# Gated linear attention with a SiLU MLP on one core: opening re-ordered by half groups, weights behind the first inputs, logs a group ahead

## The chip, the cores and the metric

The kernel runs on one core of a Trainium2 chip. The metric is the device time of one execution in microseconds (us), lower is better. Besides the runs that are timed, one execution was recorded by the hardware profiler; its times are what the rest of this text reads.

The engines by their names in the profile: PE is TensorE (matmuls), PEld its weight loads, ACT is ScalarE (activations), DVE is VectorE, POOL is GpSimd, SP is SyncE, which here only issues DMAs. POOL and ACT can issue DMAs too. Every engine works through its own instructions in the order of the program.

## The reference

Four inputs of 4 x 8 x 768 x 48 floats (batch, heads, sequence, head size) go through a recurrence with a forget gate, and its output, as 3072 rows of 384, through a two-layer MLP.

```python
f = 1.0 / (1.0 + np.exp(-f_logit))
for t in range(S):
    state = f[:, :, t, :, None] * state + np.einsum('bhd,bhe->bhde', k[:, :, t], v[:, :, t])
    y[:, :, t] = np.einsum('bhd,bhde->bhe', q[:, :, t], state)
...
h = x @ w_in
g = h * (1.0 / (1.0 + np.exp(-h)))
return (g @ w_out).astype(np.float32)
```

## The kernel before

The sequence is cut into six groups of 128 positions; a group holds these positions for all four batches and eight heads (512 rows of the MLP). In a group the recurrence is computed as attention with decays, and a state of each batch goes from one group to the next. The work of a group g:

- `load(g)` (L74): four DMAs on SP's queue, in the order f, k, q, v, each 768 KB into tiles `f_ld`, `k_ld`, `q_ld`, `v_ld`, with two buffers each. A run of 48 floats (192 bytes) is contiguous in memory.
- `prep(g)`: ACT computes `e` = exp(-f) (L127) and `lf` = ln(1 + e) (L128) for the whole group. POOL copies v into `vp` (L130). Then, for each batch b, PE sums the logs along the positions into `cs` (L135), ACT makes `a` = exp(-cs) and `ia` = exp(cs) (L137, L139), DVE makes `qg` = q times `a` (L140), POOL makes `ki` = k times `ia` (L141). At the end PE sums the logs over the group (`al_ps`, L146) and ACT takes `al` of them (L150). Tiles `a` and `ia` have two buffers.
- `attend(g)`, for each batch: `transposes` (PE `t_ps` L169, DVE `qk` L171), `scores` (PE `a_ps` L179, DVE `atm` L183), `outputs` (PE `y_ps` L198, DVE `xT` L199) and `state` (PE `d_ps` L206 and L209, DVE `st` L213).
- `mlp_in(g)`: 16 tiles of three matmuls into `h_ps` (L240), each followed by ACT's SiLU into `hT` (L243). `mlp_out(g)`: 64 matmuls into `o_ps` (L250), DVE's copy to `o_sb` (L255), and the DMA out (L257).

Exp, Ln and SiLU each need their table on ACT; a change of table is an ACT_TABLE_LOAD in the profile.

The order on every engine is the order of the code, since the schedule is written by hand: `interleave` takes the next step of whichever stream has spent the smaller share of its stated cost. Ahead of the loop stand the constants, the clearing of `lf`, `qg`, `ki` (POOL, L94 to L96), `vp` and `st` (DVE, L97, L99), the two weight DMAs on POOL's queue (L102 `w_in_sb`, L104 `w_out_sb`), `load(1)`, `prep(0)`, and `attend(0)` interleaved with `prep(1)`. Then the loop over g: `load(g + 2)`; `mlp_in(g)` interleaved with the first half of `attend(g + 1)`; `mlp_out(g)` interleaved with its second half and with `prep(g + 2)`.

In PSUM one pool of three buffers, `acc`, holds `cs`, `al_ps`, `y_ps` and `d_ps` in turn; `t_ps` and `a_ps` have one buffer each; `h_ps` and `o_ps` share two.

Of the kernel before, what the change touches and what calls it, by code (L numbers as in the profile page):

```python
# [17 lines left out]
def interleave(*streams):  # L18


    live = [[g, float(total), 0.0] for g, total in streams]
    while live:
        s = min(live, key=lambda s: s[2] / s[1])
        try:
            s[2] += next(s[0])
        except StopIteration:
            live.remove(s)


@with_exitstack  # L30
def kernel(
# [10 lines left out]
    nc = tc.nc  # L42
# [17 lines left out]
    acc = ctx.enter_context(tc.tile_pool(name="acc", bufs=3, space=PSUM))  # L60
# [4 lines left out]
    def group_view(t, g):  # L65
        return t.rearrange("b h s d -> s (b h) d")[g * C:(g + 1) * C]

    loaded = {}

    def load(g):  # L70
        tiles = {}
        for name, src in (("f", f_logit), ("k", k), ("q", q), ("v", v)):
            t = ld.tile([C, B, H, D], F32, name=f"{name}_ld", tag=f"{name}_ld")
            nc.sync.dma_start(out=t.rearrange("p b h d -> p (b h) d"), in_=group_view(src, g))  # L74
            tiles[name] = t
        loaded[g] = tiles

    load(0)
# [9 lines left out]
    lf = [singles.tile([C, B, H, 64], BF16, name=f"lf{i}") for i in range(2)]  # L88
# [4 lines left out]
    for i in range(2):  # L93
        nc.gpsimd.memset(lf[i], 0.0)  # L94
        nc.gpsimd.memset(qg[i], 0.0)
        nc.gpsimd.memset(ki[i], 0.0)  # L96
        nc.vector.memset(vp[i], 0.0)  # L97
    for b in range(B):
        nc.vector.memset(st[b], 0.0)  # L99

    w_in_sb = singles.tile([128, KT, d_ff], BF16)
    nc.gpsimd.dma_start(out=w_in_sb, in_=moe_w_in.rearrange("(ko ki) n -> ki ko n", ki=128))  # L102
    w_out_sb = singles.tile([128, NT, d_model], BF16)
    nc.gpsimd.dma_start(out=w_out_sb, in_=moe_w_out.rearrange("(ko ki) n -> ki ko n", ki=128))  # L104

    load(1)

    def v_head(g, b, h):
        return 128 + h * VW

    def v_window(g, b, h, t):
        lo = v_head(g, b, h) - (h * D - t * 128)
        return vp[g % 2][:, b, lo:lo + 128]

    def st_block(b):
        base = st[b].rearrange("p n w -> p (n w)")
        return base

    alast = {}
    prepped = {}  # L120

    def prep(g):

        t = loaded.pop(g)
        i = g % 2
        e = gk.tile([C, B, H, D], F32, name="e")
        nc.scalar.activation(e, t["f"], AF.Exp, scale=-1.0)  # L127
        nc.scalar.activation(lf[i][:, :, :, 0:D], e, AF.Ln, bias=1.0)  # L128
        for b in range(B):
            nc.gpsimd.tensor_copy(  # L130
                vp[i][:, b, 128:].rearrange("p (h w) -> p h w", w=VW)[:, :, 0:D], t["v"][:, b])
        yield 0.0
        for b in range(B):
            cs = acc.tile([C, H, D], F32, name="cs", tag="acc")
            nc.tensor.matmul(cs, triu, lf[i][:, b, :, 0:D], start=True, stop=True)  # L135
            a = wk.tile([C, H, D], F32, name="a")
            nc.scalar.activation(a, cs, AF.Exp, scale=-1.0)  # L137
            ia = wk.tile([C, H, D], F32, name="ia")
            nc.scalar.activation(ia, cs, AF.Exp, scale=1.0)  # L139
            nc.vector.tensor_mul(qg[i][:, b, :, 0:D], t["q"][:, b], a)  # L140
            nc.gpsimd.tensor_mul(ki[i][:, b, :, 0:D], t["k"][:, b], ia)  # L141
            yield 162.0
        al_ps = acc.tile([C, B, NP], F32, name="al_ps", tag="acc")
        for b in range(B):
            for p in range(NP):
                nc.tensor.matmul(al_ps[:, b, p:p + 1], lf[i][:, b, 2 * p:2 * p + 2, :], ones,  # L146
                                 start=True, stop=True)
            yield 160.0
        al = gk.tile([C, B, NP], F32, name="al")
        nc.scalar.activation(al, al_ps, AF.Exp, scale=-1.0)  # L150
        alast[g] = al
        yield 0.0

    PREP = 4 * 162.0 + 4 * 160.0

    xT = {}

    def attend(g):
        i = g % 2
        x = gk.tile([128, KT, B, C], BF16, name="xT")  # L160
        xT[g] = x
        qk = {}
        atm = {}

        def transposes(b):
            t_ps = tps.tile([128, 2, NP, C], BF16, name="t_ps")
            for j, src in ((0, qg), (1, ki)):
                for p in range(NP):
                    nc.tensor.transpose(t_ps[:, j, p, :], src[i][:, b, 2 * p:2 * p + 2, :], ident)  # L169
            sb = wk.tile([128, 2, NP, C], BF16, name="qk")  # L170
            nc.vector.tensor_copy(sb, t_ps)  # L171
            qk[b] = sb

        def scores(b):
            a_ps = aps.tile([C, 2, NP, C], F32, name="a_ps")
            for p in range(NP):
                for r in range(2):
                    lo = 64 * r
                    nc.tensor.matmul(a_ps[:, r, p, :], qk[b][lo:lo + D, 1, p, :], qk[b][lo:lo + D, 0, p, :],  # L179
                                     start=True, stop=True)  # L180
            sb = wk.tile([C, 2, NP, C], BF16, name="atm")
# [141 lines left out]
```

## Time and profile before

| | |
|---|---|
| median of three runs | 272.38 us (271.5 to 273.1) |
| the profiled execution | 272.63 us |
| its span, first to last instruction | 270.6 us |
| mean granted TensorE clock | 0.943 |
| busy: PE, ACT, DVE, POOL | 197.8, 125.3, 108.1, 49.3 us |
| read from and written to memory | 25.17 MB and 4.72 MB |

The profiled execution's time is 2.0 us more than its span. How to read the views used below: the slices cut the span into 40 equal parts and give busy tenths of each engine. The chain that ended last goes back from the last instruction, at each step to what released it; in order of time it reads as the path on which the end depends. The timeline gives instructions in order (start, duration, engine, line, operation), and in brackets how long the engine stood idle before them and what released it. The view by windows gives, for a stretch, its length, then busy time of PE, PEld, DVE, ACT, POOL with instruction counts, the granted TensorE clock (1.00 is full), the DMA share and GB/s. The groups by line give shapes, counts, busy time and mean ns of one.

### The profile page before, as it was taken

The numbers are of one execution on the slowest core, as the hardware profiler recorded it, in microseconds if no ns is written. First come the engines' busy times: TensorE is split into PE (matmuls) and PEld (weight loads), VectorE is DVE, ScalarE is ACT, GpSimd is POOL, SyncE is SP. The second block draws the span as 40 slices with busy tenths as digits, with TensorE's granted clock in tenths as the row PEclk, the third lists the DMA queues.
The fourth block names the chain that finished last, engine by engine and source line by source line (L and its number), as shares of the span: only waits on it lengthen the run. The fifth ranks groups of instructions, "written<-read, shape, count | busy, mean of one in ns | idle before, by whom it ended". The sixth has DMA issues, their size and how long they took to land.

```text
span 270.6 us, 3905 instructions
## 1 busy us (share of the span) xinstructions
PE 197.8 (73%) x1616; PEld 117.7 (44%) x1632; DVE 108.1 (40%) x191; ACT 125.3 (46%) x184; POOL 49.3 (18%) x64
## 2 busy tenths in 40 slices
PE   0120003567993999975999939999849999999995
PEld 0010002455552575542664525755426655664352
DVE  7420020965243555432743434644327443720011
ACT  1910039023669415678236695156783266105700
POOL 9900070260200410004400006200044000000000
PEclk9999999995997799997999977999959999999999
DMA  9999999999000015991119980159920100011011
GB/s 145 186 207 191 184 200 186 187 183 189 7 1 0 33 58 112 167 197 23 51 39 201 187 109 29 39 115 187 189 26 30 61 29 4 0 61 58 0 48 69
DMA packets 104626, 26.99 MB, mean 100 GB/s; under 512 B 99104, under 2 KB 104224, under 8 KB 104608
## 3 DMA queue, kind: packets, MB, share of 16 engines
q1 hardware_dynamic: 102144, 23.60, 55.9%
q0 software_dynamic: 2464, 3.15, 6.6%
q8 instruction: 12, 0.20, 0.4%
q14 instruction: 6, 0.05, 0.1%
HBM read 25.17 MB, written 4.72 MB: 110 GB/s over the span
## 4 chain that ended last, share of the span: by engine, by line
PE 64%; SPq 15%; ACT 9%; DMA 4%; DVE 4%; issue 1%; POOL 1%; POOLq 0%
PE o_ps L250 25%; PE h_ps L240 23%; SPq L74 15%; PE y_ps L198 6%; DMA v_ld<-in_v_dram 4%; PE t_ps L169 4%; PE a_ps L179 2%; ACT lf L128 2%; ACT e L127 2%; ACT L128 2%; ACT L127 2%; PE cs L135 2%; DVE atm L183 1%; DVE qk L171 1%; PE d_ps L206 1%
## 5 line engine op out<-in xcount | busy, mean ns | idle before, releaser
L243 ACT ACTIVATE hT<-h_ps 128x512 bf16<-128x512 f32 x96 | 57.3, 597 | 45.7 <-PE h_ps L240 43.8
L250 PE MATMUL o_ps<-w_out_sb,hT 128*128 128x384 bf16 x384 | 77.3, 348 | 0.0
L240 PE MATMUL h_ps<-xT,w_in_sb 128*128 128x512 bf16 x272 | 73.1, 383 | 1.4 <-issue 0.2
L250 PEld LDWEIGHTS <-hT 128*128 128x128 bf16 x384 | 37.3, 103 | 44.4 <-issue 26.4
L140 DVE TENSOR_TENSOR qg<-q_ld,a 128x384 bf16<-128x384 f32 x24 | 15.1, 632 | 60.3 <-ACT a L137 48.3
L240 PEld LDWEIGHTS <-w_in_sb 128*128 128x128 bf16 x288 | 25.8, 98 | 27.5 <-issue 5.9
L135 PE MATMUL cs<-lf,triu 128*128 128x384 bf16 x24 | 10.0, 434 | 37.2 <-ACT lf L128 35.3
L171 DVE COPY qk<-t_ps 128x1024 bf16<-128x1024 bf16 x24 | 16.6, 691 | 45.0 <-PE y_ps L198 38.0
L130 POOL CAST vp<-v_ld 128x384 bf16<-128x384 f32 x24 | 11.5, 519 | 125.7 <-DMA v_ld<-in_v_dram 125.7
L183 DVE TENSOR_TENSOR atm<-a_ps,triu 128x512 bf16<-128x512 f32 x48 | 30.8, 684 | 4.9 <-PE a_ps L179 4.7
L141 POOL TENSOR_TENSOR ki<-k_ld,ia 128x384 bf16<-128x384 f32 x24 | 24.3, 1022 | 33.5 <-ACT ia L139 33.5
L169 PE MATMUL t_ps<-ident,ki 128*128 128x128 bf16 x96 | 10.5, 238 | 21.5 <-POOL ki L141 21.5
L255 DVE COPY o_sb<-o_ps 128x384 f32<-128x384 f32 x24 | 13.4, 558 | 29.5 <-PE o_ps L250 29.2
L198 PE MATMUL y_ps<-atm,vp 128*128 128x128 bf16 x240 | 23.5, 231 | 1.2 <-DVE xT L199 1.1
L139 ACT ACTIVATE ia<-cs 128x384 f32<-128x384 f32 x24 | 11.7, 486 | 25.1 <-POOL ki L141 24.9
L137 ACT ACTIVATE a<-cs 128x384 f32<-128x384 f32 x24 | 11.8, 491 | 20.8 <-PE cs L135 18.9
L213 DVE TENSOR_TENSOR st<-d_ps,al 48x192 bf16<-48x192 f32 x40 | 14.1, 353 | 14.1 <-PE d_ps L209 13.8
L198 PEld LDWEIGHTS <-vp 128*128 128x128 bf16 x240 | 17.6, 104 | 1.8 <-issue 1.6
L150 ACT ACTIVATE al<-al_ps 128x16 f32<-128x16 f32 x6 | 1.1, 183 | 34.4 <-PE al_ps L146 34.4
L169 PEld LDWEIGHTS <-ki 128*128 128x128 bf16 x96 | 7.3, 107 | 21.7 <-POOL ki L141 21.7
L198 PE MATMUL y_ps<-qk,st 128*128 128x128 bf16 x120 | 16.5, 219 | 0.0
L169 PEld LDWEIGHTS <-qg 128*128 128x128 bf16 x96 | 8.1, 106 | 17.6 <-issue 12.4
(34 smaller groups left out, 152.1 us busy)
## 6 DMA issues: line engine op xcount, KB each, us to landing
f_ld<-in_f_logit_dram SPq DMA_DIRECT2D x6, 768.0 KB, 6.9
k_ld<-in_k_dram SPq DMA_DIRECT2D x6, 768.0 KB, 10.3
q_ld<-in_q_dram SPq DMA_DIRECT2D x6, 768.0 KB, 10.9
v_ld<-in_v_dram SPq DMA_DIRECT2D x6, 768.0 KB, 11.2
out_dram<-o_sb SPq DMA_DIRECT2D x24, 192.0 KB, 1.9
w_in_sb<-in_moe_w_in_dram POOLq DMA_DIRECT2D x1, 1536.0 KB, 11.6
w_out_sb<-in_moe_w_out_dram POOLq DMA_DIRECT2D x1, 1536.0 KB, 21.5
```

What stands on the lines that cost most here:

```text
L74: nc.sync.dma_start(out=t.rearrange("p b h d -> p (b h) d"), in_=group_view(src, g))
L135: nc.tensor.matmul(cs, triu, lf[i][:, b, :, 0:D], start=True, stop=True)
L140: nc.vector.tensor_mul(qg[i][:, b, :, 0:D], t["q"][:, b], a)
L141: nc.gpsimd.tensor_mul(ki[i][:, b, :, 0:D], t["k"][:, b], ia)
L169: nc.tensor.transpose(t_ps[:, j, p, :], src[i][:, b, 2 * p:2 * p + 2, :], ident)
L171: nc.vector.tensor_copy(sb, t_ps)
L183: nc.vector.tensor_mul(sb[:, r], a_ps[:, r], triu[:, None, :].to_broadcast([C, NP, C]))
L198: nc.tensor.matmul(y_ps[:, t, :], l, r, start=(n == 0), stop=(n == len(terms) - 1))
L213: nc.vector.tensor_mul(blocks[lo:lo + D, :, r * D:(r + 1) * D], d_ps[lo:lo + D, :, r * D:(r + 1) * D], alast[g][lo:lo + D, b, :, None].to_ ...
L240: nc.tensor.matmul(h_ps, w_in_sb[:, kk, n * 128:(n + 1) * 128], xT[g][:, kk].rearrange("p b c -> p (b c)"), start=(kk == 0), stop=(kk == K ...
L243: nc.scalar.activation(hT[g][:, n, :], h_ps, AF.Silu)
L250: nc.tensor.matmul(o_ps, hT[g][:, n, b * C:(b + 1) * C], w_out_sb[:, n, :], start=(n == 0), stop=(n == NT - 1))
```

## The change

1. **Loads.** `load` takes a group, a name and a range of batches. Group 0 is loaded in two halves (batches 0 and 1, then 2 and 3); f and q of it are issued by SP, k and v by ACT. From group 2 on, f of a group is loaded an iteration ahead of its k, q and v.
2. **Weights.** The two weight DMAs become four (512 columns of `w_in` each) and two (half of `w_out` each), and POOL issues them later in its order, `w_in` behind the second half's `ki`, `w_out` behind its `vp`.
3. **Clearing.** Only the last 16 of 64 columns of `lf`, `qg`, `ki` are cleared, by DVE; `st` and the second `vp` are cleared by POOL behind the weight DMAs.
4. **Order of group 0.** Its `prep` and `attend` run by halves, without interleaving with group 1; its `state` steps are interleaved with `prep(1)`.
5. **Logs a group ahead.** `logs(g)` (`e` and `lf`) is taken out of `prep`, and runs on ACT behind the second phase of iteration g - 3 (`lf` gets a third buffer). For group 2 it runs at the start of the second phase of iteration 0, and there `prep(2)` starts only when 5000 of its 6250 cost units have passed.
6. **In `prep`.** `ia` comes before `a`; `vp` and `ki` alternate on POOL; all `al_ps` matmuls stand together.
7. **PSUM.** `acc` (3) is split into `cps` (1 buffer for `cs` and `al_ps`) and `yps` (2 for `y_ps` and `d_ps`). Tile `qk` gets a third buffer.
8. **Stated costs** of the attend steps change from 560, 450, 1100, 450 to 450, 350, 900, 330.

The diff, cut to this:

```diff
-    acc = ctx.enter_context(tc.tile_pool(name="acc", bufs=3, space=PSUM))
+    cps = ctx.enter_context(tc.tile_pool(name="cps", bufs=1, space=PSUM))
+    yps = ctx.enter_context(tc.tile_pool(name="yps", bufs=2, space=PSUM))
...
+    def load(g, name, b0=0, b1=B, eng=None):
+        if (g, name) not in loaded:
+            loaded[g, name] = ld.tile([C, B, H, D], F32, name=f"{name}_ld", tag=f"{name}_ld")
+        t = loaded[g, name]
+        src = SRC[name].rearrange("b h s d -> s (b h) d")[g * C:(g + 1) * C, b0 * H:b1 * H]
+        (eng or nc.sync).dma_start(out=t[:, b0:b1].rearrange("p b h d -> p (b h) d"), in_=src)
+
+    HB = B // 2
+    for lo, hi, names in ((0, HB, "fkqv"), (HB, B, "fkqv")):
+        for name in names:
+            load(0, name, lo, hi, nc.scalar if name in "kv" else nc.sync)
...
+    def load_w_in():
+        src = moe_w_in.rearrange("(ko ki) n -> ki ko n", ki=128)
+        for n in range(0, d_ff, 512):
+            nc.gpsimd.dma_start(out=w_in_sb[:, :, n:n + 512], in_=src[:, :, n:n + 512])
...
+    def logs(g, lo, hi):
...
+        nc.scalar.activation(e[:, lo:hi], f[:, lo:hi], AF.Exp, scale=-1.0)
+        nc.scalar.activation(lf[g % 3][:, lo:hi, :, 0:D], e[:, lo:hi], AF.Ln, bias=1.0)
+
+    def decay(g, b):
+
         i = g % 2
...
+        cs = cps.tile([C, H, D], F32, name="cs", tag="cs")
+        nc.tensor.matmul(cs, triu, lf[g % 3][:, b, :, 0:D], start=True, stop=True)
+        ia = wk.tile([C, H, D], F32, name="ia")
+        nc.scalar.activation(ia, cs, AF.Exp, scale=1.0)
+        nc.gpsimd.tensor_mul(ki[i][:, b, :, 0:D], loaded[g, "k"][:, b], ia)
+        a = wk.tile([C, H, D], F32, name="a")
+        nc.scalar.activation(a, cs, AF.Exp, scale=-1.0)
+        nc.vector.tensor_mul(qg[i][:, b, :, 0:D], loaded[g, "q"][:, b], a)
...
+    def prep(g, wait):
+
+        yield wait
+        for b in range(B):
+            values(g, b)
+            decay(g, b)
+            yield 200.0
+        lasts(g)
+        yield 450.0
...
     with tc.manual_schedule():
...
+        logs(0, 0, 1)
+        logs(0, 1, HB)
+        for half in range(2):
+            mine = range(half * HB, half * HB + HB)
+            if half:
+                logs(0, HB, B)
+            for b in mine:
+                decay(0, b)
+            for b in mine:
+                transposes(0, b)
+            if half:
+                load_w_in()
+            for b in mine:
+                values(0, b)
+            for b in mine:
+                scores(0, b)
+            if half:
+                load_w_out()
+                pads(lf[1], qg[1], ki[1], lf[2])
+                for b in range(B):
+                    nc.gpsimd.memset(st[b], 0.0)
+                nc.gpsimd.memset(vp[1], 0.0)
+                for name in "fkqv":
+                    load(1, name)
+            for b in mine:
+                outputs(0, b)
+        lasts(0)
+        logs(1, 0, B)
+        for _ in interleave_gen((prep(1, 0.0), prep_cost(0.0)), (chain(*[once(state, 0, b) for b in range(B)]), B * 330.0)):
             pass
...
+        load(2, "f")
+
         for g in range(NCH):
             if g + 2 < NCH:
...
+                for name in "kqv":
+                    load(g + 2, name)
+            if g + 3 < NCH:
+                load(g + 3, "f")
...
             if g + 2 < NCH:
...
+                wait = 0.0
+                if g == 0:
+                    logs(2, 0, B)
+                    wait = 5000.0
+                second.append((prep(g + 2, wait), prep_cost(wait)))
...
+            if g + 3 < NCH:
+                logs(g + 3, 0, B)
```

**ACT in the opening.** The rows of ACT's order from the start of the program, before; `lf_105` is the `lf` of group 0, the numbers mark buffers.

```order
L127 ACT_TABLE_LOAD
L127 ACTIVATE e<-f_ld 128x1536
L128 ACT_TABLE_LOAD
L128 ACTIVATE lf_105<-e 128x32x48
L137 ACT_TABLE_LOAD
L137 ACTIVATE a<-cs 128x384
L139 ACTIVATE ia<-cs 128x384
```

And now, from the same place (`lf_112` is group 0's):

```order
L85 DMA k_ld<-in_k_dram 128x16x48
L85 DMA v_ld<-in_v_dram 128x16x48
L85 DMA k_ld<-in_k_dram 128x16x48
L85 DMA v_ld<-in_v_dram 128x16x48
L142 ACT_TABLE_LOAD
L142 ACTIVATE e<-f_ld 128x384
L143 ACT_TABLE_LOAD
L143 ACTIVATE lf_112<-e 128x8x48
L142 ACT_TABLE_LOAD
L142 ACTIVATE e<-f_ld 128x384
L143 ACT_TABLE_LOAD
L143 ACTIVATE lf_112<-e 128x8x48
```

Four DMA issues now stand ahead of ACT's first table load, and the first half's logs are taken batch by batch, with four table loads where one pair stood.

**POOL in the opening.** Before, behind the constants (`vp_111` and `ki_109` belong to group 0):

```order
L94 MEMSET lf_105 128x2048
L95 MEMSET qg_107 128x2048
L96 MEMSET ki_109 128x2048
L94 MEMSET lf_106 128x2048
L95 MEMSET qg_108 128x2048
L96 MEMSET ki_110 128x2048
L102 DMA w_in_sb<-in_moe_w_in_dram 128x3x2048
L104 DMA w_out_sb<-in_moe_w_out_dram 128x16x384
L130 CAST vp_111<-v_ld 128x8x48 x4
L141 TENSOR_TENSOR ki_109<-k_ld,ia 128x8x48 x4
```

And now (`ki_117`, `vp_119` of group 0, `vp_120` of group 1):

```order
L152 TENSOR_TENSOR ki_117<-k_ld,ia 128x8x48 x2
L158 CAST vp_119<-v_ld 128x8x48 x2
L152 TENSOR_TENSOR ki_117<-k_ld,ia 128x8x48 x2
L119 DMA w_in_sb<-in_moe_w_in_dram 128x3x512 x4
L158 CAST vp_119<-v_ld 128x8x48 x2
L124 DMA w_out_sb<-in_moe_w_out_dram 128x8x384 x2
L324 MEMSET st_121 128x1536
L324 MEMSET st_122 128x1536
L324 MEMSET st_123 128x1536
L324 MEMSET st_124 128x1536
L325 MEMSET vp_120 128x6144
L158 CAST vp_120<-v_ld 128x8x48
```

The weight DMAs moved behind both halves' `ki`, and five memsets stand between them and the first work on group 1.

**ACT in a middle iteration.** Before, behind the sixteen SiLUs of `mlp_in(1)`, up to those of `mlp_in(2)` (`lf_106` is group 3's):

```order
L243 ACTIVATE hT<-h_ps 128x512 x16
L127 ACT_TABLE_LOAD
L127 ACTIVATE e<-f_ld 128x1536
L128 ACT_TABLE_LOAD
L128 ACTIVATE lf_106<-e 128x32x48
L137 ACT_TABLE_LOAD
L137 ACTIVATE a<-cs 128x384
L139 ACTIVATE ia<-cs 128x384
```

And now, the end of the same stretch (`lf_113` is now group 4's), behind the four pairs of `ia` and `a` of `prep(3)`:

```order
L151 ACTIVATE ia<-cs 128x384
L154 ACTIVATE a<-cs 128x384
L167 ACTIVATE al<-al_ps 128x16
L142 ACTIVATE e<-f_ld 128x1536
L143 ACT_TABLE_LOAD
L143 ACTIVATE lf_113<-e 128x32x48
L261 ACT_TABLE_LOAD
L261 ACTIVATE hT<-h_ps 128x512 x16
```

The logs moved from between the SiLUs and the exponentials of the same `prep` to between the last exponential and the next group's SiLUs, for the group after.

256 lines of the change are left out of this document (119 added, 137 removed).

## The prediction

> **What bounds the kernel now.** I read the slices first, then the chain in order of time, then the windows by stage, then single rows. The slices of the granted clock and of DMA:
>
> ```profile
> PEclk9999999995997799997999977999959999999999
> DMA  9999999999000015991119980159920100011011
> ```
>
> A slice is 6.8 us. DMA is full for ten slices, to 68 us, and later only in bursts. The clock dips after the opening and again once in every group. The chain says what the first 64 us are:
>
> ```profile
> 0.74 0.43 SPq L74
> ...
> 1.23 3.09 SPq L74
> ...
> 12.76 15.56 SPq L74
> ...
> 40.97 10.99 DMA v_ld<-in_v_dram
> ...
> 52.53 1.74 POOL vp L130 x3
> 54.27 0.97 POOL ki L141
> ...
> 64.27 0.59 PE h_ps L240
> ```
>
> SP's issues stall (0.43 us for the first, up to 15.56 later) until v of **group 1** lands at 51.96; then 12.3 us of one group's preparation run until the first `h_ps` at 64.27 (call this start S). From there the stages, each ending where the next group's `h_ps` begins:
>
> ```profile
> 36.00:52.10 16.10, 5.74 (x49) 4.02 (x50) 6.23 (x10) 9.09 (x13) 5.24 (x8) 1.00 1.45 187
> 64.30:103.50 39.20, 34.05 (x278) 20.18 (x282) 17.21 (x34) 22.00 (x32) 5.83 (x8) 0.88 0.17 33
> 103.50:140.80 37.30, 32.25 (x277) 19.35 (x280) 16.97 (x33) 21.31 (x32) 5.83 (x8) 0.95 0.65 107
> 140.80:178.50 37.70, 32.65 (x277) 19.42 (x280) 17.05 (x33) 21.32 (x32) 5.90 (x8) 0.91 0.68 105
> 178.50:216.20 37.70, 32.62 (x278) 19.49 (x281) 17.05 (x33) 21.39 (x32) 5.83 (x8) 0.91 0.68 105
> 216.20:245.10 28.90, 28.05 (x238) 16.85 (x241) 12.07 (x21) 9.76 (x17) 0.00 (x0) 1.00 0.08 29
> 245.10:270.60 25.50, 22.07 (x110) 10.56 (x109) 2.55 (x5) 9.56 (x16) 0.00 (x0) 1.00 0.10 39
> ```
>
> PE fills the later stages, except for one hole in each of the four groups that prepare another. That of the second, from ACT's and PE's timelines:
>
> ```profile
> 118.44 0.60 ACT L243 ACTIVATE hT<-h_ps 128x512 bf16<-128x512 f32 x1 [0.49 <-PE h_ps L240]
> 119.06 1.28 ACT L127 ACT_TABLE_LOAD   x1
> 120.35 1.48 ACT L127 ACTIVATE e<-f_ld 128x1536 f32<-128x1536 f32 x1
> 121.85 1.28 ACT L128 ACT_TABLE_LOAD   x1
> 123.15 1.48 ACT L128 ACTIVATE lf<-e 128x1536 bf16<-128x1536 f32 x1
> ...
> 124.68 0.32 PE L135 MATMUL cs<-lf,triu 128*128 128x384 bf16 x1 [4.73 <-ACT lf L128]
> 124.84 2.32 PE L250 MATMUL o_ps<-w_out_sb,hT 128*128 128x384 bf16 x8
> ...
> 127.28 1.49 PE L250 MATMUL o_ps<-w_out_sb,hT 128*128 128x384 bf16 x4
> 128.56 0.40 PE L206 MATMUL d_ps<-st,ident 128*128 128x384 bf16 x1
> ...
> 256.73 10.45 PE o_ps L250 x64
> ```
>
> PE stands 4.73 us at `cs` for the logs, and is slow behind it: the twelve `o_ps` took 2.1 and 1.3 us where 64 of them take 10.45, so 12 take 1.96; with two `cs` that is 1.7 us lost. A group without hole is therefore 37.3 - 4.7 - 1.7 = **30.9 us**. The 28.9 of the stage at 216.2, with no `prep` or state, is the cross-check.
>
> **The change, part one: the start S.** Three chains end there; none is simply removed.
>
> *Data.* Up to the last byte of group 1 the same bytes must move. The first 12 us ran at 163 GB/s and later ones at 187, so data begin at about 1.5 us:
>
> ```profile
> 0.00:12.00 12.00, 0.74 (x3) 0.50 (x4) 8.09 (x7) 6.31 (x5) 11.43 (x14) 1.00 1.18 163
> ...
> q0 software_dynamic: 959, 0.74, 93.5%
> q1 hardware_dynamic: 956, 0.18, 33.5%
> ```
>
> A 768 KB load is 4.2 us at 187 GB/s, a group 16.8; group 0 lands at 18.3. To 51.96 before, that leaves 51.96 - 1.5 - 33.6 = 16.9 us for the weights. The last two rows are the weight queue and the input queue in the stretch 24 to 29 us: both move the same number of packets, so they alternate, and a weight packet is many times larger. Now `w_in` is cut into runs of 512 columns: 1536 + 2048 = 3584 weight packets, beside which 3584 input packets of 192 bytes (3.7 us alone) pass. If POOL issues the weights at T, group 1 has had T - 18.3 of its 16.8 us. For T = 31, 4.1 us are left, more than 3.7: all weights go first, and v lands at 52 as before. For T = 33, 2.1 us are left (2050 packets), v lands at 33 + 2.1 + 16.9 x 2050/3584 = 45; from T = 35 on, at once. So **later weights bring S forward**.
>
> As to ACT as a second issuer: the DMA share was 1.45 on one queue already. The Trainium skill ("DMA: Bandwidth & Descriptors", Issuing engines are not separate DMA queues) says that DMAs started on several engines run on the same engines and interleave; by it the second queue brings nothing, against some 8 us earlier for group 0 if it doubled the rate. The full share speaks for the rule. My sum goes by the share alone.
>
> *ACT and PE.* Durations, from the groups by line:
>
> ```profile
> L141 POOL TENSOR_TENSOR ki<-k_ld,ia 128x384 bf16<-128x384 f32 x24 | 24.3, 1022 | 33.5 <-ACT ia L139 33.5
> ...
> L130 POOL CAST vp<-v_ld 128x384 bf16<-128x384 f32 x24 | 11.5, 519 | 125.7 <-DMA v_ld<-in_v_dram 125.7
> ...
> L183 DVE TENSOR_TENSOR atm<-a_ps,triu 128x512 bf16<-128x512 f32 x48 | 30.8, 684 | 4.9 <-PE a_ps L179 4.7
> ...
> L140 DVE TENSOR_TENSOR qg<-q_ld,a 128x384 bf16<-128x384 f32 x24 | 15.1, 632 | 60.3 <-ACT a L137 48.3 <-DMA q_ld<-in_q_dram 11.8
> ...
> L139 ACT ACTIVATE ia<-cs 128x384 f32<-128x384 f32 x24 | 11.7, 486 | 25.1 <-POOL ki L141 24.9
> L135 PE MATMUL cs<-lf,triu 128*128 128x384 bf16 x24 | 10.0, 434 | 37.2 <-ACT lf L128 35.3 <-ACT ia L139 1.1 <-DVE xT L199 0.8
> ...
> L94 POOL MEMSET lf<- 128x2048 bf16 x2 | 3.6, 1796 | 0.0
> ...
> L102 POOL DMA_DIRECT2D w_in_sb<-in_moe_w_in_dram x1 | 0.9, 931 | 0.0
> ```
>
> ACT's four issues block it until its ring takes them. Bounds: 2 us (a first issue on SP takes 0.43 us) and 14 us (the pace of the data); I take 7.5, since SP's second issue waited 3 us. Then per batch of the first half two table loads (1.28) and two activations of about 0.45: to 14.4. Table load, `ia`, `a`, `cs`, `ia`, `a`: to 18.1. From there DVE and PE for two batches: `qg`, `qk`, transposes, `qk`, scores, `atm` pair, scores, `atm` pair, outputs, eight steps of 0.6 to 1.4: the second half's `cs` at 26. Its table load waits for it; then 4.2 us to the last `ki`: **T = 31**. Behind this the second half's attention ends at 38, and only then ACT takes the logs of group 1 (4.4 us with the Ln load): 43. `prep(1)`, four `cs` one after another through one PSUM buffer, 1.4 us each, with the table load, ends near **52**.
>
> *POOL.* At T it issues `w_in` four times (0.93 each), copies `vp`, issues `w_out` twice (taken alike), then clears 4 x 1536 + 6144 columns at 1.796 us for 2048: 10.8 us, until 48.4. Two `vp` and `ki` pairs for group 1 (3.1), the last `ia` and `a`, `al_ps` and a state (2.0): **53.5**. Data, with v at 52, gives 52 + 3.1 + 2.0 = **57**, or 50 with v at 45. I take S = **55**, near the middle of 52, 53.5 and 57. Bounds: 50 (late weights and an ACT freed at 2 us) and 60 (ACT freed at 14). Gain 9.3.
>
> **Part two: the four groups** (39.2 + 37.3 + 37.7 + 37.7 = 151.9).
>
> ```profile
> 105.72 1.29 PE h_ps L240 x6
> ...
> 131.84 0.89 PE y_ps L198 x16
> ```
>
> - *Groups 2 and 3* find their logs ready. In place of the hole ACT's Exp table load now waits for the first `cs`: 1.28 + 0.39 + 0.49 = 2.2 us until the one `cs` buffer is free, while PE has eight `o_ps` (1.3): 1.0 us is left, 31.9 each. The logs stand behind `al`: 1.5 + 1.3 + 1.5 + 1.3 = 5.6 us on ACT, and the first SiLU must end (0.6) before the third `h_ps` tile finds a buffer. Until there PE has 20 `o_ps` (3.3), an `y_ps` (0.9), a `d_ps` (0.5), two `h_ps` tiles (1.3) and their transposes (0.9): 6.9 against 6.2, covered, barely.
> - *Group 0*: `prep(2)` is pressed into the last fifth of the second phase. There `cs` waits for `ia` and `a` of the one before: 1.6, 1.1, 0.4 and 0.5 us, 3.6 together, and the cold start of before (1.5, from 39.2 against 37.7) stays, with 0.5 for slow matmuls: 36.5.
> - *Group 1* starts with ACT still at the logs of group 3 (5.6 us behind `al`), and `h_ps` has two buffers: PE has four `o_ps`, two `h_ps` tiles and two transposes (2.8), then waits, with DVE's copies between, 3.5 us for the first SiLU. With 1.5 for the clock behind it and 1.0 as above: 36.9.
>
> As to that 1.5: the clock behind the 4.73 us was
>
> ```profile
> 125.00:130.00 5.00, 5.00 (x30) 2.55 (x28) 2.29 (x5) 2.70 (x6) 2.64 (x4) 0.66 0.02 5
> ```
>
> The Trainium skill ("TensorE: Matmul & The Clock Gate", What's actually happening) says the clock halves after at least one idle window of about 3.4 us, which runs freely. By it the row is explained, waits of 1 us cost nothing more, and one of 3.5 us may or may not: the sum would be 1.5 lower if it does not.
>
> Sum 36.5 + 36.9 + 31.9 + 31.9 = 137.2; gain 14.7. The last two stages (54.4) hold the same work: nothing.
>
> **Total**: 55 + 137.2 + 54.4 = 246.6 of span, plus 2.0 around it (272.63 against 270.6): **249 us**. The profiled execution stands 0.25 us over the median of 272.38, which I neglect.
>
> **The rivals.**
> - *An early opening*: T falls to 33 or later, or group 1 comes in ahead of the weights; then the chains of 50 to 52 decide, and short waits leave the clock alone: 249 - 5 - 3 = 241. For it: the steepness above. Against: POOL's memsets alone reach 48.4. Chance 0.15.
> - *The opening is not shortened*: POOL's six issues or ACT's four block longer than I took; S stays near 64, 258 in all. For it: SP's issue of 15.56 us in the chain. Against: the one large weight issue took 0.93 us. Chance 0.15.
> - *The logs do not leave the path* (the change doesn't do what it says): the cover of 6.9 us against 6.2 fails, and groups 2 and 3 also start with a wait for SiLU, 3.5 + 1.5 each: 259. Chance 0.10.
> - *Slower*: with the holes gone, PE runs densely from S on, and the granted clock sinks under the load. 191.6 us follow S; the gain of 24 is gone when they stretch by 24/191.6, a mean clock of 0.89; at 0.85 the time is 249 + 34 = 283. For it: 0.88 to 0.95 in the groups. Against: the last 54 us, with PE busy 28.05 of 28.9 us, ran at 1.00, and the dips lie behind holes. Chance 0.04.
>
> **How the numbers follow.** The forecast has 0.56. The range goes from 240 (the early case) to 259 (the two late ones); the slower case and the far ends stay out. A difference of 0.5% (1.4 us, about the spread of the runs) is what can be told from no change. Faster 0.95, same 0.02, slower 0.03 (of the 0.04 a little falls into no change, and the late cases stay faster).
>
> **What would show it.** Right: first `h_ps` at 52 to 58; no 4.7 us hole at `cs`; waits of about 1 us at the second `cs` of groups 2 and 3; a wait of 3 to 4 us for SiLU at the start of group 1; weights issued near 31; v of group 1 near 50. Wrong: ACT's first `e` later than 14 us, POOL standing in its DMA issues, or `h_ps` waits at the starts of groups 2 and 3.

## The result: the profile after

| | before | after |
|---|---|---|
| median of the runs | 271.94 us (271.06 to 273.10) | 252.75 us (249.62 to 252.91) |
| ratio, 95% interval | | 0.9265 [0.9183, 0.9346] |
| the profiled execution | 272.63 us | 252.69 us |
| its span | 270.6 us | 250.9 us |
| mean granted TensorE clock | 0.943 | 0.984 |

The prediction was 249, with a range of 240 to 259. Where the runs of a kernel fell into a fast and a slow state, as in one experiment below, its ratio is that of the fast runs alone. The slices of the granted clock and of DMA after the change (6.3 us each):

```profile
PEclk9999999999999999599999999999999999999998
DMA  9999999999980107992017993159801100110011
```

DMA is full for eleven slices, to 69 us (the weights now come last), and of four dips of the clock behind holes one is left, near 100 us. (Up to 61.8 us the trace has no record of the clock, and the view puts 1.00 there; the last section comes back to this.) The windows by stage, cut at each group's first `h_ps` (length; busy time of PE, PEld, DVE, ACT, POOL; granted clock; DMA share; GB/s):

```profile
0.00:58.04 58.04, 17.14 (x160) 12.25 (x162) 22.81 (x37) 25.73 (x36) 27.93 (x34) 1.00 1.33 182
58.04:94.48 36.44, 32.57 (x277) 19.73 (x279) 18.44 (x34) 21.29 (x32) 7.23 (x9) 1.00 0.60 95
94.48:132.50 38.02, 33.57 (x279) 19.79 (x280) 18.70 (x34) 23.62 (x33) 8.03 (x10) 0.91 0.64 105
132.50:164.40 31.90, 30.57 (x280) 18.75 (x281) 18.37 (x33) 19.91 (x31) 6.81 (x8) 1.00 0.80 124
164.40:196.30 31.90, 30.57 (x279) 18.75 (x281) 18.38 (x33) 17.11 (x29) 6.81 (x8) 1.00 0.61 100
196.30:225.30 29.00, 28.68 (x240) 17.17 (x243) 12.91 (x22) 9.55 (x16) 0.00 (x0) 1.00 0.08 28
225.30:250.90 25.60, 21.96 (x110) 10.48 (x108) 2.44 (x5) 9.56 (x16) 0.00 (x0) 0.97 0.11 39
```

Read the lengths against the prediction's terms. S came at 58.04 for 55; groups 0 to 3 took 36.44, 38.02, 31.90 and 31.90 for 36.5, 36.9, 31.9 and 31.9; the last two stages 54.6 for 54.4. The chain in order of time (start, duration, what) says what the first stage was made of:

```profile
0.74 0.49 ACTq L85
1.26 2.07 ACTq L85
3.36 4.87 ACTq L85
8.26 4.45 ACTq L85
12.74 1.28 ACT L142
...
36.32 0.91 POOL w_in_sb L119 x2
...
42.18 5.34 POOL st L324 x4
47.52 5.16 POOL vp L325
52.75 0.76 POOL vp L158
...
58.04 1.06 PE h_ps L258 x2
```

ACT's four DMA issues hold it until 12.74; then comes the chain of decays and scores; POOL issues the weights, clears `st` and `vp` for 10.5 us, and only then works on group 1. No DMA stands in the chain any longer: v of group 1 (issued at 25.34, landed 11.1 us later) is there long before POOL comes to it at 52.75. The idle times of PE, from its timeline, which were 4.73 us in each of four groups:

```profile
89.41 0.32 PE L149 MATMUL cs<-lf,triu 128*128 128x384 bf16 x1 [1.65 <-ACT a L154]
90.75 0.32 PE L149 MATMUL cs<-lf,triu 128*128 128x384 bf16 x1 [1.02 <-ACT a L154]
92.09 0.32 PE L149 MATMUL cs<-lf,triu 128*128 128x384 bf16 x1 [0.37 <-ACT a L154]
93.44 0.54 PE L164 MATMUL al_ps<-ones,lf 128*128 128x1 bf16 x16 [0.69 <-ACT a L154]
...
100.32 2.72 PE L258 MATMUL h_ps<-xT,w_in_sb 128*128 128x512 bf16 x6 [3.19 <-ACT hT L261]
...
119.94 0.32 PE L149 MATMUL cs<-lf,triu 128*128 128x384 bf16 x1 [1.00 <-ACT a L154]
```

and three windows around the 3.19:

```profile
99.00:99.50 0.50, 0.00 (x0) 0.00 (x0) 0.00 (x0) 0.50 (x1) 0.00 (x0) 0.88 1.40 218
100.30:105.30 5.00, 4.98 (x22) 2.02 (x22) 1.29 (x2) 1.94 (x4) 0.00 (x0) 0.50 1.45 188
106.00:106.50 0.50, 0.50 (x3) 0.25 (x2) 0.50 (x1) 0.00 (x0) 0.00 (x0) 0.80 1.44 196
```

Group 0 waits 3.73 us in four pieces at its packed `prep(2)`; group 1 waits 3.19 for the first SiLU. The clock is at half speed from 99.38 (0.88 over the first window), while PE still waits, to 106.2 (0.80 over the last): 6.8 us. Groups 1 to 3 keep a wait of 1.00 at the second `cs`.

### The profile page after: what moved, and what is told of

Same layout as the page of the kernel before. It is cut to its first block, busy times and chain, and to the rows that moved or that the text cites. A ratio compares the mean times of both kernels' runs of the same rounds, so it can differ in the third digit from the quotient of the medians.

```text
span 250.9 us, 3936 instructions
## 1 busy us (share of the span) xinstructions
PE 195.1 (78%) x1616; PEld 116.9 (47%) x1632; DVE 112.0 (45%) x193; ACT 126.8 (51%) x189; POOL 56.8 (23%) x67
## 4 chain that ended last, share of the span: by engine, by line
PE 69%; ACT 13%; POOL 7%; ACTq 5%; DVE 3%; issue 2%; POOLq 0%
PE h_ps L258 26%; PE o_ps L268 23%; PE y_ps L209 8%; ACTq L85 5%; PE t_ps L179 4%; ACT L151 3%; PE a_ps L189 3%; ACT ia L151 3%; PE cs L149 2%; POOL st L324 2%; POOL vp L325 2%; ACT a L154 2%; ACT L143 2%; PE d_ps L223 1%; DVE atm L193 1%
## 5 line engine op out<-in xcount | busy, mean ns | idle before, releaser
L258 PE MATMUL h_ps<-xT,w_in_sb 128*128 128x512 bf16 x272 | 75.1, 393 | 4.4 <-ACT hT L261 3.2
L268 PE MATMUL o_ps<-w_out_sb,hT 128*128 128x384 bf16 x384 | 71.1, 326 | 0.0
L268 PEld LDWEIGHTS <-hT 128*128 128x128 bf16 x384 | 35.6, 98 | 26.6 <-issue 5.4
L155 DVE TENSOR_TENSOR qg<-q_ld,a 128x384 bf16<-128x384 f32 x24 | 21.9, 913 | 41.1 <-ACT a L154 41.1
L149 PE MATMUL cs<-lf,triu 128*128 128x384 bf16 x24 | 9.1, 378 | 39.6 <-ACT lf L143 20.9
L152 POOL TENSOR_TENSOR ki<-k_ld,ia 128x384 bf16<-128x384 f32 x24 | 25.3, 1054 | 64.0 <-ACT ia L151 64.0
L158 POOL CAST vp<-v_ld 128x384 bf16<-128x384 f32 x24 | 16.2, 681 | 69.6 <-DMA v_ld<-in_v_dram 69.5
L212 DVE CAST xT<-y_ps 128x384 bf16<-128x384 f32 x24 | 13.2, 553 | 12.5 <-PE y_ps L209 12.5
L179 PE MATMUL t_ps<-ident,qg 128*128 128x128 bf16 x96 | 10.9, 245 | 3.7 <-DVE qk L181 2.1
L189 PE MATMUL a_ps<-qk 48*128 48x128 bf16 x192 | 10.6, 236 | 2.9 <-DVE atm L193 2.9
## 6 DMA issues: line engine op xcount, KB each, us to landing
q_ld<-in_q_dram SPq DMA_DIRECT2D x5, 768.0 KB, 11.1
v_ld<-in_v_dram SPq DMA_DIRECT2D x5, 768.0 KB, 11.1
```

The costliest lines, as they stand in the source:

```text
L152: nc.gpsimd.tensor_mul(ki[i][:, b, :, 0:D], loaded[g, "k"][:, b], ia)
L155: nc.vector.tensor_mul(qg[i][:, b, :, 0:D], loaded[g, "q"][:, b], a)
L158: nc.gpsimd.tensor_copy(v_data(g % 2, b), loaded[g, "v"][:, b])
L189: nc.tensor.matmul(a_ps[:, r, p, :], qkT[b][lo:lo + D, 1, p, :], qkT[b][lo:lo + D, 0, p, :], start=True, stop=True)
L258: nc.tensor.matmul(h_ps, w_in_sb[:, kk, n * 128:(n + 1) * 128], xT[g][:, kk].rearrange("p b c -> p (b c)"), start=(kk == 0), stop=(kk == K ...
L268: nc.tensor.matmul(o_ps, hT[g][:, n, b * C:(b + 1) * C], w_out_sb[:, n, :], start=(n == 0), stop=(n == NT - 1))
```

## The experiments

Twelve kernels were run, in four lots, each beside the kernel before. "Changed kernel" is the one above. "S" is the start of the first `h_ps`.

### All first loads on SP's queue

```diff
-            load(0, name, lo, hi, nc.scalar if name in "kv" else nc.sync)
+            load(0, name, lo, hi)
```

> All eight loads of group 0 on SP, so ACT is free at once instead of at 12.74 us and its first exponential can start near 4.2 us (14.03 in the changed kernel). Theory A (the weights' place among the bytes counts): the weights are issued near 26.5 instead of 36.3, group 1 has then had 8 of its 16.8 us, all weights go ahead of its v, which lands near 52 instead of 36; POOL's first copy of group 1 moves from a wait on its own clears to a wait on v at about 52, and the first h_ps stays at 57 to 58: 252 us. Theory B (the chain of ACT and POOL alone sets the opening, and it starts 10 us earlier): first h_ps near 48, 243 us.

Measured: 252.13 us, ratio 0.9269 [0.9216, 0.9321]; the changed kernel's 0.9265 lies within this interval. S is at 58.50. POOL's timeline (in brackets: idle before, and releaser):

```profile
26.98 3.24 POOL L119 DMA_DIRECT2D w_in_sb<-in_moe_w_in_dram  x4
...
53.47 0.50 POOL L158 CAST vp<-v_ld 128x384 bf16<-128x384 f32 x1 [10.06 <-DMA v_ld<-in_v_dram]
```

ACT is free from the start, the weights are issued at 26.98 instead of 36.26, and so they overtake group 1: POOL, done with its clears at 43.4, stands idle for 10.06 us until v lands. What ACT gained, the order of transfers took back. Theory A holds: ACT's blocking, which delays the weights, and early weights, which delay v, give the same S by two chains.

### POOL's clears first

The five clears of `st` and `vp[1]` move from behind the weight DMAs to the start of the program.

```diff
+        for b in range(B):
+            nc.gpsimd.memset(st[b], 0.0)
+        nc.gpsimd.memset(vp[1], 0.0)
         logs(0, 0, 1)
```

> POOL's clears of st and of the second vp (10.5 us between the weights' issue and group 1's first copy) are put at the start of the program, where POOL is idle. Theory A: behind them ACT's chain stands almost level (logs of group 1 only at 43.9, then cs, Exp table and four ia, a pairs through one PSUM buffer), so the first h_ps moves only from 58.0 to about 56.6: 251.3 us. Theory B: the clears are the bound of the opening, first h_ps near 48 to 50, 243 us.

Measured: 249.66 us, 0.9164 [0.9109, 0.9218], S at 56.78. The chain in order of time:

```profile
44.17 1.37 ACT e L142
...
56.78 1.06 PE h_ps L258 x2
```

Taking 10.5 us off POOL's chain moves S by 1.3: the next chain, ACT's logs of group 1 and its decays, had ended only that much ahead of POOL's. That is theory A.

### Weights held behind the clears, without ACT's issues

The first experiment's line, and POOL's values and clears ahead of the weight DMAs:

```diff
-            if half:
-                load_w_in()
...
+            if half:
+                for b in range(B):
+                    nc.gpsimd.memset(st[b], 0.0)
+                nc.gpsimd.memset(vp[1], 0.0)
+                load_w_in()
...
```

> As e1 (all loads of group 0 on SP, ACT free at once), and POOL's clears now stand ahead of the weight DMAs instead of behind them, so the weights are issued near 38.5 us instead of 27. Theory A (bytes: weights issued behind the last byte of group 1 let v of group 1 land near 36): the 10 us of the earlier ACT chain are now kept; first h_ps near 48.5 us, 243 us. Theory B (holding the weights only moves the wait onto them): w_in is late, PE waits for it, first h_ps at 53 or later, 248 us or more.

Measured: 242.87 us, 0.8918 [0.8870, 0.8967]. The chain in order of time:

```profile
28.41 5.27 POOL st L318 x4
33.68 2.83 POOL vp L319
...
39.71 2.32 POOL w_in_sb L119 x3
```

and in PE's timeline the first `h_ps`:

```profile
49.18 1.06 PE L258 MATMUL h_ps<-xT,w_in_sb 128*128 128x512 bf16 x2 [0.22 <-issue]
```

The clears now fill the time in which group 1 lands, the weights follow, and S falls to 49.18. Each half alone (the first experiment's ACT, the second's clears) gave 0 and 1.3 us; both together, with the weights issued behind the clears, give 8.9. Theory A holds.

### Weights behind the first inputs, alone

In the kernel before, the two weight DMAs move behind `ki` of group 0; nothing else changes.

```diff
-    nc.gpsimd.dma_start(out=w_in_sb, in_=moe_w_in.rearrange("(ko ki) n -> ki ko n", ki=128))
...
-    nc.gpsimd.dma_start(out=w_out_sb, in_=moe_w_out.rearrange("(ko ki) n -> ki ko n", ki=128))
...
         for _ in prep(0):
             pass
+        nc.gpsimd.dma_start(out=w_in_sb, in_=moe_w_in.rearrange("(ko ki) n -> ki ko n", ki=128))
+        nc.gpsimd.dma_start(out=w_out_sb, in_=moe_w_out.rearrange("(ko ki) n -> ki ko n", ki=128))
```

> The kernel before with only the two weight DMAs moved behind the ki of group 0 in POOL's order (issued near 25 us instead of 12). Theory A (bytes): v of group 0 is used near 19 instead of 35, but v of group 1 still lands near 52, since the same bytes go ahead of it, and group 1's preparation follows as before; first h_ps at 61 to 64: 269 to 272 us. Theory B (the start of group 0 sets the opening): first h_ps near 50, 257 us.

Measured over ten runs: 273.09 us, 1.0017 [0.9987, 1.0048]: no difference. POOL's timeline:

```profile
19.80 1.85 POOL L128 CAST vp<-v_ld 128x384 bf16<-128x384 f32 x4 [7.68 <-DMA v_ld<-in_v_dram]
...
53.42 1.85 POOL L128 CAST vp<-v_ld 128x384 bf16<-128x384 f32 x4 [25.57 <-DMA v_ld<-in_v_dram]
```

v of group 0 is used at 19.80, that of group 1 at 53.42 (51.96 was its landing before), since the weights, issued at 25.7, still overtake it. S, at 65.28, needs group 1, so the early group 0 buys nothing: theory A, a little past its upper ends (64 and 272 us).

### Logs a group ahead, alone

In the kernel before, with its three `acc` buffers and its opening; the loads of f run an iteration ahead.

```diff
+    def logs(g):
+        e = gk.tile([C, B, H, D], F32, name="e")
+        nc.scalar.activation(e, loaded[g]["f"], AF.Exp, scale=-1.0)
+        nc.scalar.activation(lf[g % 3][:, :, :, 0:D], e, AF.Ln, bias=1.0)
...
+                if g == 0:
+                    logs(2)
+                    wait = 5000.0
...
+            if g + 3 < NCH:
+                logs(g + 3)
```

> The kernel before with only the logs a group ahead (third lf buffer, f loaded ahead, the same 5000 units for prep(2)); al_ps stays in four steps that end with the group. Theory A (it is the place of al in the group that lets the logs hide): the logs stand behind al, which comes 1 us before the group's end, so 5.6 us of ACT fall on the next group's first SiLUs: a wait of 3 to 4 us and a slow clock there in the place of the 4.7 us hole; 268 to 273 us. Theory B (taking the logs out of prep is enough): the holes of groups 1 to 3 vanish, 255 us.

Measured: 0.9507 [0.9419, 0.9594], some 13 us less than before (runs from 257.54 to 262.65 us; the profiled one took 257.54). The windows of groups 0 to 3:

```profile
63.86:95.66 31.80, 30.84 (x278) 18.91 (x282) 17.43 (x31) 20.82 (x31) 4.93 (x7) 1.00 0.40 70
95.66:131.85 36.19, 32.07 (x278) 18.97 (x280) 18.68 (x35) 20.59 (x32) 7.62 (x10) 0.95 0.68 110
131.85:166.94 35.09, 31.90 (x278) 18.89 (x280) 17.52 (x33) 19.81 (x31) 5.88 (x8) 0.95 0.73 113
166.94:200.77 33.83, 30.64 (x279) 18.69 (x280) 17.53 (x33) 19.80 (x31) 5.88 (x8) 1.00 0.57 94
```

and PE's timeline:

```profile
101.92 2.25 PE L246 MATMUL h_ps<-xT,w_in_sb 128*128 128x512 bf16 x6 [2.85 <-ACT hT L249]
137.35 2.72 PE L246 MATMUL h_ps<-xT,w_in_sb 128*128 128x512 bf16 x6 [2.86 <-ACT hT L249]
```

The hole at `cs` goes, and a wait of 2.85 for SiLU takes its place in the next group, groups 2 and 3 too, where the changed kernel has none: what the rival "the logs do not leave the path" foresaw. Theory A had the new wait, but longer, and did not count that group 0 falls from 39.2 to 31.8. So the result lies between the theories. The four groups take 136.9 us here, 151.9 before and 138.3 in the changed kernel: the logs alone are worth all that the change gained in the groups. Which other edit gave the changed kernel its cover in groups 2 and 3 was not tried alone; it is not the split of PSUM, since with that undone (below) both take 30.74.

### `prep(2)` spread instead of packed

```diff
-                    wait = 5000.0
+                    wait = 600.0
```

> prep(2) starts after 600 of 1850 cost units of the second phase instead of 5000 of 6250. Theory A (the packed cs waits of 3.7 us in group 0, and the 3.2 us wait for SiLU with 2 to 3 us of half clock behind it in group 1, both come from where prep(2) ends): waits in group 0 fall to about 2 us, the SiLU wait of group 1 to about 1 us without a slow clock: 6 us less, near 246.5 us. Theory B (group 1 is slow for another reason, such as the loads of 96 to 110 us beside it): 1.5 us less at most, 251 us.

Measured: 246.0 us, 0.9049 [0.8995, 0.9102]. PE's timeline:

```profile
83.66 0.32 PE L149 MATMUL cs<-lf,triu 128*128 128x384 bf16 x1 [0.75 <-ACT a L154]
96.17 1.46 PE L258 MATMUL h_ps<-xT,w_in_sb 128*128 128x512 bf16 x6 [1.56 <-ACT hT L261]
```

and the windows of groups 0 and 1:

```profile
58.18:91.96 33.78, 32.17 (x278) 19.64 (x280) 19.94 (x35) 22.91 (x33) 8.00 (x10) 1.00 0.60 102
91.96:125.58 33.62, 30.73 (x279) 18.77 (x281) 18.38 (x33) 22.01 (x32) 6.82 (x8) 1.00 0.73 118
```

Group 0 gets 2.7 us shorter, and its waits fall from 3.73 us to 1.46. Group 1 gets 4.4 shorter: ACT is done earlier, the wait for SiLU is 1.56 instead of 3.19, and the clock stays at 1.00 (PE busy for 30.73 us instead of 33.57). Theory A holds. One number in the order was worth 6 to 7 us.

### PSUM split undone

`cs`, `al_ps`, `y_ps` and `d_ps` share one pool of three again.

```diff
-    cps = ctx.enter_context(tc.tile_pool(name="cps", bufs=1, space=PSUM))
-    yps = ctx.enter_context(tc.tile_pool(name="yps", bufs=2, space=PSUM))
+    acc = ctx.enter_context(tc.tile_pool(name="acc", bufs=3, space=PSUM))
```

> The changed kernel with the PSUM split undone (one pool of three for cs, al_ps, y_ps, d_ps). Theory A (the single cs buffer is what packed cs steps wait for): the waits at cs fall from 3.7 us to about 1 in group 0 and from 1.0 to 0 in groups 1 to 3; part of group 0's comes back as a longer wait for SiLU in group 1, since ACT's exponentials still take their time; 4 us less in all, 248.5 us. Theory B (the split helps: y_ps and d_ps no longer wait behind cs): 254 us or more.

Measured: 245.98 us, 0.9027 [0.8982, 0.9072]; groups 34.86, 37.10, 30.74, 30.74, S at 57.04. PE's timeline in group 1:

```profile
95.13 0.81 PE L257 MATMUL h_ps<-xT,w_in_sb 128*128 128x512 bf16 x3 [2.19 <-DVE o_sb L272]
98.80 2.72 PE L257 MATMUL h_ps<-xT,w_in_sb 128*128 128x512 bf16 x6 [2.33 <-ACT hT L260]
```

With three buffers a `cs` need not wait for the `a` of the one before, and every stage is shorter, though group 1 waits twice. Theory A holds, with more gain than its 4 us: by stages the split cost 5.8 (1.0 before S, then 1.6, 0.9, 1.2 and 1.2).

### The exponentials' table asked for early

A `[128, 1]` exponential ahead of the second phase's `prep`, into a new 4-byte tile; no output changes.

```diff
+    tiny = singles.tile([C, 1], F32)
+
+    def exp_table():
+        nc.scalar.activation(tiny, ones, AF.Exp)
...
+                exp_table()
                 second.append((prep(g + 2, wait), prep_cost(wait)))
```

> The changed kernel with one tiny Exp on ACT at the start of each second phase, so that the Exp table is loaded before the first cs and not behind it. Theory A (the 1.0 us waits at the second cs come from the table load of 1.28 us in the 2.2 us until the one cs buffer is free): these waits vanish in groups 1 to 3, and 1.65 becomes 0.4 in group 0: 4.3 us less, 248.4 us. Theory B (ACT's pair ia, a or POOL's pace behind it sets these waits): no difference, 252 us.

Measured: 246.6 us, 0.9043 [0.8999, 0.9088]. PE's first wait in group 0, and the window of group 2:

```profile
87.17 0.32 PE L153 MATMUL cs<-lf,triu 128*128 128x384 bf16 x1 [0.37 <-ACT a L158]
128.00:158.84 30.84, 30.51 (x280) 18.74 (x280) 18.38 (x33) 20.00 (x32) 6.82 (x8) 1.00 0.64 129
```

The 1.65 in group 0 became 0.37, and the waits of 1.00 went: groups 35.74, 35.76, 30.84, 30.84. The table load now lies beside `o_ps`. Theory A holds. Groups 0, 2 and 3 gained 0.7, 1.1 and 1.1, and group 1 gained 2.3, in part by a shorter dip of the clock (0.66 over 5 us). S was also 1.5 earlier: the input ran at 221 GB/s, and ACT's four issues ended at 11.34 instead of 12.74. That has nothing to do with the table; the last experiment explains it.

### The gains together

The edits on loads, clears, weights' order, spread and table in one kernel; besides, the logs of group 1 run ahead of the last outputs of group 0, and the weights are issued between the decays of `prep(1)`.

```diff
+        logs(0, 0, HB)
...
+            if half:
+                logs(1, 0, B)
             for b in mine:
                 outputs(0, b)
...
+            if g > 1:
+                values(g, b)
+            elif b == 2:
+                load_w_in()
...
+        if g == 1:
+            for b in range(B):
+                values(1, b)
+            load_w_out()
```

> The changed kernel with the edits that gained alone put together: all first loads from SP's queue, POOL's clears at the program's start, the values and the clears ahead of the weight loads, the logs of group 0 in one go and those of group 1 ahead of the other outputs, prep of group 2 begun over the last chunks of group 1 and not packed into group 0, the exponentials' table asked for early. Theory A (the gains sit in different stages and add up): the opening ends at 42 to 44 us instead of 58.04, since the chain over the held weights (49.18 alone) now has neither the clears nor the eight decays ahead of it; groups 0 to 3 take about 33.0, 32.5, 30.9 and 30.9, the last two stages 54.6; 225 to 228 us. Theory B (a new bound gives the opening's part back: the input weight is now needed 15 us sooner, and whatever is late next, its landing or ACT, sets the start): the opening ends at 49 or later, and the time is 233 or more.

Measured: 228.4 us (227.99 to 229.02), 0.8402 [0.8356, 0.8447]. The windows of groups 0 and 1:

```profile
43.94:77.38 33.44, 32.28 (x281) 19.46 (x281) 18.52 (x31) 22.04 (x33) 8.42 (x10) 1.00 0.89 152
77.38:109.94 32.56, 30.82 (x281) 18.77 (x280) 18.37 (x33) 22.10 (x33) 6.82 (x8) 1.00 0.61 122
```

and the first `h_ps` in PE's timeline:

```profile
43.94 1.46 PE L262 MATMUL h_ps<-xT,w_in_sb 128*128 128x512 bf16 x3 [3.81 <-DMA w_in_sb<-in_moe_w_in_dram]
```

The sizes of the stages are those of A (S 43.94, groups within 0.5 us of it; the time is 0.4 over its 228), and the new bound of B is there too, but it ends 5 us before the 49 that B gave it: PE waits 3.81 us for `w_in`. This kernel holds the 4-byte tile too; the share of S that is due to it (see the last experiment) was not measured apart.

The same with one pool of three accumulators:

```diff
-    cps = ctx.enter_context(tc.tile_pool(name="cps", bufs=1, space=PSUM))
-    yps = ctx.enter_context(tc.tile_pool(name="yps", bufs=2, space=PSUM))
+    acc = ctx.enter_context(tc.tile_pool(name="acc", bufs=3, space=PSUM))
```

> The same kernel with one PSUM pool of three accumulators for the outputs, the sums of logs and the matmuls of the input weight, in place of the split by use. Theory A (the split costs in group 0, where a sum of logs waits for the decay before the one before it): waits ahead of the sums of logs go, the second group's waits for the SiLU and for an accumulator grow, as they did with the pool of three alone; within 2 us of the kernel with the split, 224 to 229. Theory B (with preps apart from group 0 the three accumulators clash in the second group): that group takes over 36 us with a granted clock under 0.95, and the time is 3 us or more above the kernel with the split.

Measured: 227.97 us (227.50 to 228.65), 0.8380 [0.8340, 0.8421]; from the kernel with the split it can't be told apart. So the 5.8 us of the split do not come on top of the other gains: with `prep(2)` spread, the table early and S set by `w_in` (PE waits 4.96 us for it here, S is 44.09), the split costs nothing that can be told. Which of the three makes it harmless was not tried. These two kernels are faster than both the kernel before and the changed one.

### Where the load tiles stand in SBUF

From 3 to 23 us the three kernels with the 4-byte tile had loaded at 220 or 221 GB/s; the seven others that moved nothing but inputs then (the changed kernel among them), at 189. In the programs as built the tile takes 32 bytes, and the load tiles behind it move from 32 bytes off a multiple of 64 onto one. To separate this from the exponential, the kernel with all loads on SP's queue got a tile that is only cleared:

```diff
     w_out_sb = singles.tile([128, NT, d_model], BF16)
+    gap = singles.tile([C, 1], F32)
+    nc.vector.memset(gap, 0.0)
```

> The kernel with all first loads on SP's queue, and a 4-byte tile cleared by DVE that stands ahead of the load tiles in SBUF: they move by 32 bytes per partition, so that every run of 192 bytes lands at a multiple of 64 bytes (before, in the changed kernel and in the experiments that loaded at 187 GB/s they began 32 bytes off such a multiple; in the two runs that showed 217 to 221 GB/s, both with a 4-byte tile added for another purpose, on one). Theory A (the alignment sets the rate of the short runs): the first 20 us load at 216 to 222 GB/s instead of 187, the input of two groups (6.3 MB) takes about 5 us less, v of group 1 lands at 46 to 49 instead of 53.35, and the start of the first matmul of the MLP, which waits for it in this kernel, comes at 51 to 54 instead of 58.50: 245 to 248 us against 252.1. Theory B (the higher rate came from elsewhere: the chip, chance, or the activation that used the tile): 187 GB/s, 58.5, 252 us.

and in a second kernel `[C, 16]`, 64 bytes, by which the load tiles stand off again:

> The same with a tile of 64 bytes in place of the one of 4: the load tiles move by 64 bytes per partition and stand 32 bytes off a multiple of 64 again. Theory A (alignment): as without the tile, 187 GB/s, v of group 1 at 53, 252 us. Theory C (any shift, or the added instruction, does it): as with the tile of 4 bytes.

Measured: 241.81 us, 0.8841 [0.8771, 0.8911], with 4 bytes; 250.94 us, 0.9197 [0.9155, 0.9239], with 64. The window from 3 to 23 us, first with 4, then with 64 bytes:

```profile
3.00:23.00 20.00, 6.87 (x55) 4.66 (x55) 8.90 (x12) 12.32 (x16) 3.23 (x4) 1.00 1.24 221
```

```profile
3.00:23.00 20.00, 6.87 (x55) 4.66 (x55) 8.80 (x12) 11.90 (x16) 3.22 (x4) 1.00 1.39 188
```

and in POOL's timeline the first use of v of group 1, first with 4, then with 64 bytes:

```profile
43.28 0.76 POOL L160 CAST vp<-v_ld 128x384 bf16<-128x384 f32 x1
...
53.41 0.50 POOL L160 CAST vp<-v_ld 128x384 bf16<-128x384 f32 x1 [9.77 <-DMA v_ld<-in_v_dram]
```

The same engines do the same work at 221 against 188 GB/s. With 4 bytes POOL does not wait for v at all, and S is 48.16 (58.02 with 64 bytes): earlier than A's 51 to 54, since v is there before the clears end, and POOL's clears are the bound. v gains far more than the rate alone gives: issued at 22.45, it landed 9.3 us later, near 31.8, instead of at 53.3. This is the prediction's steepness: at the higher rate little of group 1 is left when the weights are issued (26.80). A place in SBUF was worth 9 us.

## Why the prediction came out as it did

- **S, 55 against 58.04.** The term that was mis-sized is ACT's blocking by its four issues, 7.5 us taken (bounds 2 and 14), 12.74 measured; ACT's first `e` came at 14.03, just past the 14 that the prediction had named as a sign of being wrong. The rest of that chain stands: 5.2 us later, the weights should be issued at 36.2 (36.26 measured), and POOL's chain should end at 53.5 + 5.2 = 58.7 (58.04 measured).
- **That 55 was near has luck in it.** A start that needs three chains comes with the latest, and with the prediction's own T = 31 that was data, 57; it took 55, near the middle. The data chain was not there at all: v of group 1 landed at 36.4, not near 50 as the signs have it, and POOL's chain, longer than taken, ended close to where the data chain would have.
- **"Later weights bring S forward."** The rule itself held: issued at 36.26, they no longer delay v; issued at 26.98, they put it at 53.4. But the slip that frees the data is the same slip that delays POOL and ACT, so S stayed at 58 either way. The prediction had both chains; that they trade against each other through one cause it did not say. Holding the weights without delaying ACT (49.18) is what the rival of an early opening needed.
- **The second issuer.** The prediction took no rate from it, and none came: from 3 to 23 us the input ran at 189 GB/s with two issuers, and at 189 with all loads on SP. The Trainium skill ("DMA: Bandwidth & Descriptors", Issuing engines are not separate DMA queues) says so, and adds that only the issuing time is saved, which is usually small. The first half agrees. The second does not hold here: an issue of 0.49 us was followed by ones of 2.07, 4.87 and 4.45 on ACT.
- **Groups 2 and 3.** 31.9 forecast, 31.90 measured, with the wait of 1.0. Asking for the table early removed that wait, which shows its cause.
- **Group 0.** 36.5 against 36.44; waits of 1.6, 1.1, 0.4 and 0.5 forecast, 1.65, 1.02, 0.37 and 0.69 measured.
- **Group 1.** 36.9 against 38.02. The wait was 3.19 for 3.5; the clock's share was mis-sized: half speed lasted 6.8 us, and PE was busy for 33.57 us where the same work took 30.57 in group 2, so it cost 3.0 and not 1.5. The Trainium skill ("TensorE: Matmul & The Clock Gate", What's actually happening) puts the idle window at about 3.4 us, free-running. The traces agree on steps of that length, but no step had to be idle to its end: the clock fell 2.25 us into the wait of 3.19. The length of a wait alone does not decide either: two waits of 2.86 us with the logs alone were followed by 0.74 and by 1.00 over 5 us, the second at 172.45. The last section has what does go with it.
- **Rivals.** "The opening is not shortened" had the right mechanism for ACT; of the 9 us that it put on S, 3 came. "The logs do not leave the path" did not come, but does where the logs move alone. "Slower" did not come: groups 2 and 3 run dense at a clock of 1.00.

In sum: 3.0 us from S, 1.1 from group 1 and 0.2 from the last stages make 250.9 of span for 246.6.

## What to carry to other kernels

An issue behind others lasts as long as the data take to flow: two of SP's loads of 768 KB held it for 4.16 us each (at 21.14 and 25.34), which is their time at 189 GB/s, and ACT's four issues ended 1.4 us earlier when the same input ran at 221. So the price of issuing from an engine that also computes is the pace of the data, and not the 0.49 us of a first issue. And where two orders of transfers trade one chain for another, moving one alone shows nothing (0.0 for the loads on SP, no gain for the weights alone, 8.9 us together with the clears). Work moved off a path must not be packed together elsewhere: with the logs moved alike, `prep(2)` packed at the end of a phase cost 6 to 7 us more than spread over it. And for short runs, look at where the destination tiles begin before believing that a full DMA share is the limit.

## What the runs showed that was not expected

The rate of 192-byte runs into SBUF depends on the tile's start: 188 GB/s 32 bytes off a multiple of 64, 221 on one, with the DMA share falling from 1.39 to 1.24. The prediction had read a share of 1.45 as the limit of the engines. Whether it is the start alone, or that every run begins and ends on a multiple, was not separated.

The clock looked odd at one place: behind the 3.81 us wait for `w_in` the view reads 1.00, yet three `h_ps` took 1.46 us, where three take 0.81 at 77.38. That 1.00 is no reading. The trace's records of the clock begin at 47.1 us in that kernel, where the matmuls become fast; in the changed kernel they begin at 61.8, and three `h_ps` at 59.75 took 1.49. So the mean clocks of two traces cover different parts of the opening, and are a poor comparison.

The records also show what goes with a dip. In all 14 traces the clock changes only at whole multiples of 3.41 us from the first record. Of 738 such steps at full clock, 26 were followed by half clock; PE had stood idle for 2.00 us or more in each of these, and for 1.96 at most in each of the other 712. In the changed kernel the step that ends at 99.38 holds 2.31 us of idle time. The same wait can therefore give no step of half clock or more than one: behind 3.19 us there were two in the changed kernel, and one with the clears first, where group 1 took 36.6 us instead of 38.0. A difference of 1 or 2 us between two of these kernels may be no more than where the steps fell. That the idle share of a step is what the clock follows is read from these traces; no kernel was made to test it.
